# A decode kernel of four layers: the last 128 outputs of wo and w4 as one full block instead of two half blocks

## The chip, the cores and the metric

The kernel runs on one core of a Trainium2 chip. Its time is the device time of that core in microseconds (us), as the median of several runs; lower is better. A profile of one execution of the program goes with it. The engines are TensorE (PE for its matmuls, PEld for its weight loads), VectorE (DVE), ScalarE (ACT), GpSimd (POOL) and SyncE (SP), which issues the loads. Sixteen DMA engines move the data.

## The reference

Eight rows of a batch (B = 8, one token each, D = 448 features) pass through four layers: attention, mixer with MLP, attention, mixer with MLP. The attention has 16 query heads of 256 features on 8 key and value heads of 4096 positions; caches and weights are the same in both passes.

```python
def _A_ref(x, k_cache, v_cache, wq, wo):
    q = (x @ wq).reshape(B, Sq, Hq, Dh).transpose(0, 2, 1, 3)
    k = jnp.repeat(k_cache, rep, axis=1)
    v = jnp.repeat(v_cache, rep, axis=1)
    p = _softmax(jnp.einsum("bhqd,bhkd->bhqk", q, k) * (Dh ** -0.5), axis=-1)
    o = jnp.einsum("bhqk,bhkd->bhqd", p, v)
    return o.transpose(0, 2, 1, 3).reshape(B, Sq, Hq * Dh) @ wo

def _B_ref(x, w1, w2, w3, w4):
    ...
    x1 = x + hs
    return x1 + _gelu(_layernorm(x1, axis=-1) @ w3) @ w4

x = x + _A_ref(_layernorm(x), A_k_cache, A_v_cache, A_wq, A_wo)
x = x + _B_ref(_layernorm(x), B_w1, B_w2, B_w3, B_w4)
x = x + _A_ref(_layernorm(x), A_k_cache, A_v_cache, A_wq, A_wo)
x = x + _B_ref(_layernorm(x), B_w1, B_w2, B_w3, B_w4)
```

With one token the kernel treats the mixer's shifted part hs as zero, so w1 and w2 aren't read. wo has 4096 rows and 448 columns, w4 has 1792 rows and 448 columns.

## The kernel before

Keys and values don't fit the on-chip memory, so both passes of attention read them from HBM, 1 MB a tile: for each batch row and each of four pairs of key and value heads (gp) four K tiles and four V tiles. Fifteen slots of 1 MB hold them. For every row eleven tiles of the first pass stay in their slots for the second pass, and a twelfth is parked in PSUM (`away`, L614, and `back`, L621), so that they are read once.

The list `items` fixes the order of all tiles of both passes; the passes of neighbouring rows are interleaved in it. For each K tile VectorE transposes the slot in place (L584), TensorE forms the scores (L594), and ScalarE takes the exponentials (L603). The transposed probabilities (L630, L637) are the weights of the PV product of each V tile (L649). After the last use of a slot, `emit_loads` lets SyncE issue the next load into it (L576); SyncE waits for the slot's last reader. Loads are issued in the order of the items.

Between the items lie the small layers of a row, written as Python generators. `step` is called twice for an item (ahead of its scores or its PV product, and after them) and advances the generators so far that `total` of their steps are spread evenly from item `at` to item `until`; the totals are written by hand in the calls of `add_gen`. A step is what lies between two `yield`s, so its instructions stand in each engine's queue where that call puts them. The generators are:

- `first_half` and `chain`, for a row after its first pass: the softmax sums and the transposed output (`half`: L412, L438, L443, L447), the product with half of wo's rows each (`add_cols`, L339), the sums into x (L468, L469), `mlp` with w3 (L357) and w4 (L339, sum at L326), and the next query (`project_q`, wq, L285).
- `first_last` and `last`: the outputs of the second pass, collected for several rows in OT2.
- `rest`: wo, w3 and w4 of rows 0 to 3 in one go (four columns a matmul), interleaved near the end.
- For rows 4 to 7, wo's product is built up in the bank `store` while the last V tiles come in (`pv_cols`, L663, then `add_cols`). The sum at L822, `mlp_hidden`, a transposition of x (L834) and w4 (L844) end the program.

x lies as columns: feature 128 f + p on partition p of column block f of the tile xT. 448 is three and a half blocks. In the kernel before, the fourth block holds features 384 to 447 twice, on partitions 0 to 63 and on 64 to 127. `rows_to_cols` (L189, L193) brings x into this form at the start. `norm` weights the sums with wv (1/448, and 0.5/448 in the fourth block, since each feature counts twice there). It writes the normalised x into xb, whose columns 3 and 4 hold the last 64 features once on the lower and once on the upper partitions, with zeros on the others (L260 for one row, L262 for more). wq and w3 store their last 64 rows split in two halves of columns, one on the lower, one on the upper partitions, and `wblk` picks column 3 or 4 accordingly. So does `add_cols`: three blocks of 128 output columns and then two of 64, both with columns 384 to 447 of the weights. Each of its matmuls loads a block of weights and multiplies one column (or four) with it:

```python
        for fc in range(5):
            lo, hi = (128 * fc, 128 * fc + 128) if fc < 3 else (384, 448)
            r = y_ps[:, fc, :] if fc < 3 else y_ps[64 * (fc - 3) : 64 * (fc - 2), 3, :]
            for i in rows:
```

It yields after every `every` blocks and after the last.

Of the kernel before, what the change touches and what calls it, by code (L numbers as in the profile page):

```python
# [17 lines left out]
def kernel(  # L18
# [27 lines left out]
    nc = tc.nc  # L46
# [86 lines left out]

    wv = consts.tile([128, 4], FP32, name="wv")
    nc.vector.memset(wv[:, 0:3], 1.0 / D)
    nc.vector.memset(wv[:, 3:4], 0.5 / D)
    one = consts.tile([128, 1], FP32, name="one")
    nc.vector.memset(one[:], 1.0)
    ones = one[:].to_broadcast([128, 128])
# [9 lines left out]
    def xbs(nb):  # L149
        return xb[1] if nb == 1 else xb[Bn][:, :, :nb]  # L150
# [33 lines left out]
    def rows_to_cols(row, nb):  # L184

        idn = identb[:nb, :nb]
        ps = room_ps("y", nb)[:, 0 : 4 * nb].rearrange("p (f b) -> p f b", b=nb)
        for fc in range(3):
            nc.tensor.matmul(  # L189
                ps[:, fc, :], row[:nb, 128 * fc : 128 * fc + 128], idn, start=True, stop=True  # L190
            )
        for r in range(2):
            nc.tensor.matmul(  # L193
                ps[64 * r : 64 * r + 64, 3, :], row[:nb, 384:448], idn, start=True, stop=True
            )
        return ps

    def norm(x, nb, twice):

        def room(name, shape, at):
            n = shape[0] * shape[1]
            if nb < Bn:
                t = chn.tile([128, n * MID], FP32, tag=name)
                ap = t[:, 0 : n * nb]
            else:
                ap = scratch(at, n * nb)
            return ap.rearrange("p (s f b) -> p s f b", s=shape[0], f=shape[1])

        def bc(ap):
            return ap.unsqueeze(1).to_broadcast([128, 4, nb])

        xx = room("xx", (2, 4), 0)
        nc.vector.tensor_mul(xx[:, 0], x, wv[:].unsqueeze(2).to_broadcast([128, 4, nb]))
        nc.vector.tensor_mul(xx[:, 1], xx[:, 0], x)
        xs = room("xs", (1, 2), 512)[:, 0]
        nc.vector.tensor_reduce(
            xs, xx.rearrange("p s f b -> p s b f"), mybir.AxisListType.X, ALU.add
        )  # L220
        yield
        st = room_ps("st", nb).rearrange("p (s b) -> p s b", b=nb)
        nc.tensor.matmul(st, ones, xs, start=True, stop=True)  # L223
        yield
        mv = room("mv", (1, 2), 528)[:, 0]
        nc.vector.tensor_copy(mv, st)
        var = room("var", (1, 1), 608)[:, 0, 0]
        if nb == 1:
            nc.vector.scalar_tensor_tensor(
                var, mv[:, 0], mv[:, 0], mv[:, 1], ALU.mult, ALU.subtract, reverse1=True  # L230
            )
        else:
            nc.vector.tensor_mul(var, mv[:, 0], mv[:, 0])
            nc.vector.tensor_sub(var, mv[:, 1], var)


        ve = room("ve", (1, 2), 544)[:, 0]
        n = 2 if twice else 1
        nc.vector.tensor_scalar(ve[:, 0], var, 0.0, EPS, ALU.max, ALU.add)
        if twice:  # L240
            nc.vector.tensor_scalar(ve[:, 1], var, 0.0, EPS * EPS / (1 + EPS), ALU.max, ALU.add)
        rs = room("rs", (1, 2), 560)[:, 0]
        nc.gpsimd.tensor_tensor(  # L243
            rs[:, 0:n].rearrange("p n b -> p (n b)"),
            ve[:, 0:n].rearrange("p n b -> p (n b)"),
            nhalf[:].to_broadcast([128, n * nb]),
            ALU.pow,
        )
        xc = room("xc", (1, 4), 576)[:, 0]
        nc.vector.tensor_tensor(xc, x, bc(mv[:, 0]), ALU.subtract)  # L250
        yield
        if nb > 1:
            yield
        c = (1 + EPS) ** -0.5 if twice else 1.0
        rl = rs[:, n - 1]
        parts = ((slice(0, 128), 0, 3, 0), (slice(0, 64), 3, 4, 3), (slice(64, 128), 3, 4, 4))
        for pp, f0, f1, to in parts:
            dst = xbs(nb)[pp, to : to + f1 - f0, :]
            if nb == 1:
                nc.vector.tensor_scalar(dst, xc[pp, f0:f1], rl[pp], c, ALU.mult, ALU.mult)  # L260
            else:
                nc.vector.scalar_tensor_tensor(  # L262
                    dst,
                    xc[pp, f0:f1],
                    c,
                    rl[pp].unsqueeze(1).to_broadcast([pp.stop - pp.start, f1 - f0, nb]),
                    ALU.mult,
                    ALU.mult,
                )
        if twice and nb == 1:  # L270
            nc.vector.scalar_tensor_tensor(x, xc, rs[:, 0], x, ALU.mult, ALU.add)
        elif twice:
            nc.vector.tensor_tensor(xc, xc, bc(rs[:, 0]), ALU.mult)
            nc.vector.tensor_add(x, x, xc)
        yield
# [51 lines left out]

    def add_cols(y_ps, rhs, w, rows, every, open=None):

        for fc in range(5):  # L330
            lo, hi = (128 * fc, 128 * fc + 128) if fc < 3 else (384, 448)
            r = y_ps[:, fc, :] if fc < 3 else y_ps[64 * (fc - 3) : 64 * (fc - 2), 3, :]
            for i in rows:
                if open is None:
                    start, stop = i == rows[0], i == rows[-1]
                else:
                    start = open[0] and fc == 0 and i == rows[0]
                    stop = open[1] and i == rows[-1]
                nc.tensor.matmul(  # L339
                    r,  # L340
                    w[:, i, lo:hi],
                    rhs(i),
                    start=start,
                    stop=stop,
                    skip_group_check=open is not None,
                )
            if fc % every == every - 1 or fc == 4:
                yield

    def mlp_hidden(b0, nb):  # L350
# [366 lines left out]
    first_of = {}  # L717
# [4 lines left out]
    for idx, it in enumerate(items):  # L722
        n, kv, c = it
        ps, b, gp = tasks[n]
        if (ps, b, gp, kv, c) == (0, Bn - 1, REST, 0, 0):
            assert pairs_done[1, MID - 1] == 4
            add_gen("rest", 0, rest(), idx + 1, idx + 18, 25)
        p = where[(b, gp), (kv, c)] if ps == 1 and (stays(it) or inside(it)) else where[it]
        slot = slots[p]
        final = (ps, b) == (1, Bn - 1)  # L730
# [33 lines left out]
        else:  # L764
# [6 lines left out]
            if final and gp in free:  # L771
                pv_cols(oc, slot, c, gp)
                if c % 2 == 1:

                    u = c // 2
                    scale_o(oc, rz_gp, gp, u, OT2[:, :, :, b])
                    h0 = 8 * gp + 4 * u
                    run(
                        add_cols(
                            st["y"],  # L780
                            lambda i: OT2[:, i % 2, i // 2, MID:],
                            wo_sb,
                            range(h0, h0 + 4),
                            5,
                            open=(claim(st), gp == free[-1] and u == 1),
                        )
                    )
            else:
                g8 = gp // 2
                if ("o", g8) not in st:  # L790
                    while len(in_use) == 2:
                        step(10 * len(items))
                    st["o", g8] = next(t for t in o_banks if all(t is not u for u in in_use))
                    in_use.append(st["o", g8])
                pv(st["o", g8], slot, c, gp, begin=(ps, b, g8) not in begun)
                begun.add((ps, b, g8))
                if ps == 0 and inside(it):
                    away(slot)
            if c == 3:
                done = pairs_done[ps, b] = pairs_done.get((ps, b), 0) + 1  # L800
                if done == 2 and ps == 0:
                    add_gen("chain", b, first_half(b, st), idx + 1, idx + 21, 11)
                elif done == 2:
                    add_gen("chain" if final else "last", b, first_last(b, st), idx + 1, idx + 13, 9)
                elif done == 4 and ps == 0:
                    add_gen("chain", b, chain(b, st), idx + 1, first_of[(1, b), 0] - 1, 40)
                elif done == 4 and not final:
                    add_gen("last", b, last(b, st), idx + 1, idx + (7 if b == Bn - 2 else 13), 6)
        if not (ps == 0 and stays(it)):
# [18 lines left out]
    run(mlp_hidden(MID, Bn - MID))  # L828
    for q in range(4):
        for fc in range(4):  # L830
            w = 128 if fc < 3 else 64
            lo, hi = max(W * q, 128 * fc), min(W * q + W, 128 * fc + w)
            if lo < hi:
                nc.tensor.matmul(  # L834
                    o_row[32 * q : 32 * q + Bn, lo - W * q : hi - W * q],
                    xT[:w, fc, :],
                    ident2[:w, lo - 128 * fc : hi - 128 * fc],
                    start=(lo == W * q),
                    stop=False,
                    skip_group_check=True,  # L840
# [47 lines left out]
```

## Time and profile before

| what | value |
|---|---|
| median of six runs | 1119.39 us (1114.99 to 1124.4) |
| the profiled execution | 1118.35 us, of it 1116.6 us span |
| mean granted TensorE clock | 0.622 of full speed |
| read from HBM | 446.77 MB, 400 GB/s over the span |
| loads of K tiles and V tiles | 200 and 216, of 1 MB each |
| median from issue to landing | 11.1 us (K), 10.6 us (V) |
| transposes of K tiles (L584), busy | 469.3 us, 400 of 1219 ns |
| scores (L594), busy | 285.3 us |
| PV products (L649), busy | 250.1 us |
| add_cols (L339), weight loads | 2230, of them 892 of 64 columns |
| SyncE's wait for slots: on L584, L649, L594 | 217.2, 208.0, 147.0 us |

Profile lines name the line of the kernel, the engine, the operation, the tiles, a count, and times in us or, where marked, ns. A time window gives the busy time of each engine in it, the granted clock, the share of the DMA engines that was busy, and the rate. The timeline merges like instructions that follow each other; what stands in brackets is the engine's idle time before them and what ended it. Matmuls are pipelined, so that their single durations overlap: how long a run of them takes is read from the length of the run.

### The profile page before, as it was taken

The page shows a single profiled execution, that of the slowest core. Times are in us where ns is not written, and L with a number is a line of the kernel's source. Part 1 is how long each engine was busy: PE and PEld are TensorE (multiplying, and loading weights), DVE is VectorE, ACT ScalarE, POOL GpSimd, SP SyncE. Part 2 cuts the span into 40 slices and gives each one's busy share as a digit, 9 for nine tenths or more (in the row PEclk, how much of TensorE's full clock was granted, in tenths as well). Part 3 has the DMA queues.
Part 4 walks back from the last instruction along what each step waited for, and adds up shares of the span by engine and source line. Part 5 has one row for each costly group of instructions (what it writes and reads, how often), then busy time and mean ns, then how long its engine had stood idle before and what let it go on. Part 6 is the DMA issues. An engine that isn't in the chain of part 4 may idle for free. (4 is left out here: it accounts for less than half of the span.)

```text
span 1116.6 us, 36998 instructions
## 1 busy us (share of the span) xinstructions
PE 714.7 (64%) x17173; PEld 517.6 (46%) x17173; DVE 591.6 (53%) x1009; ACT 124.3 (11%) x362; POOL 15.6 (1%) x25
## 2 busy tenths in 40 slices
PE   3135567756774578636865477844777477877775
PEld 2123356534552455424553255623555355655565
DVE  5155554645375564555465464655637463485462
ACT  0001001110111011100011001101111101011010
POOL 0000000000000000000000000000000000000000
PEclk9999999655565555655566555655556555565575
DMA  9999999999999999999999999999999999999994
GB/s 359 383 420 419 412 377 401 420 411 380 395 421 420 393 406 416 418 421 395 417 419 419 421 398 417 419 420 413 409 414 418 416 408 418 418 364 410 420 419 166
DMA packets 65193, 449.15 MB, mean 402 GB/s; under 512 B 6920, under 2 KB 10896, under 8 KB 11408
## 3 DMA queue, kind: packets, MB, share of 16 engines
q1 hardware_dynamic: 65008, 446.80, 98.0%
q8 instruction: 134, 2.20, 0.8%
q14 instruction: 19, 0.16, 0.0%
q10 hardware_dynamic: 32, 0.00, 0.0%
HBM read 446.77 MB, written 0.01 MB: 400 GB/s over the span
## 5 line engine op out<-in xcount | busy, mean ns | idle before, releaser
L584 DVE STREAM_TRANSPOSE slot<-slot 128x1024 uint32<-128x1024 uint32 x400 | 469.3, 1219 | 259.8 <-DMA slot<-in_A_k_cache_dram 257.3
L594 PE MATMUL sc<-slot,qbd 128*8 128x128 bf16 x8192 | 285.3, 291 | 317.0 <-DVE slot L584 249.7
L594 PEld LDWEIGHTS <-qbd 128*8 128x8 bf16 x8192 | 191.7, 107 | 388.5 <-issue 213.7
L649 PE MATMUL o<-slot,ptw 128*8 128x256 bf16 x3968 | 250.1, 396 | 39.0 <-DMA slot<-in_A_v_cache_dram 29.7
L603 ACT ACTIVATE p_n<-sc 128x256 bf16<-128x256 f32 x128 | 95.5, 746 | 806.1 <-PE sc L594 806.1
L649 PEld LDWEIGHTS <-ptw 128*8 128x8 bf16 x3968 | 112.0, 111 | 79.5 <-issue 45.5
L339 PEld LDWEIGHTS <-wo_sb 128*128 128x128 bf16 (+1 forms) x1600 | 65.4, 123 | 25.7 <-issue 25.4
L339 PE MATMUL misc<-OT,wo_sb 128*128 128x1 bf16 (+1 forms) x1280 | 58.1, 176 | 2.1 <-issue 2.1
L285 PEld LDWEIGHTS <-wq_sb 128*128 128x128 bf16 x1152 | 34.7, 104 | 24.1 <-issue 18.5
L285 PE MATMUL misc<-xb,wq_sb 128*128 128x1 bf16 x1024 | 33.5, 166 | 3.4 <-ACT ptw L637 2.8
L637 ACT CAST ptw<-misc 128x128 bf16<-128x128 f32 x64 | 17.6, 274 | 147.8 <-PE misc L630 82.5
L603 ACT ACTIVATION_READ_ACCUMULATOR p_n<-sc 128x1 f32 x128 | 33.6, 263 | 0.0
L311 DVE TENSOR_SCALAR qbd<-misc,quad 128x64 bf16<-128x64 f32 x64 | 13.8, 278 | 34.7 <-PE misc L305 34.7
L443 PEld LDWEIGHTS misc<-R,o_sb 128*128 128x128 f32 x124 | 26.9, 300 | 9.3 <-issue 7.2
L339 PEld LDWEIGHTS <-w_sb 128*128 128x128 bf16 (+1 forms) x630 | 25.0, 125 | 11.0 <-issue 11.0
L443 PE MATMUL misc<-R,o_sb 128*128 128x8 f32 x124 | 29.8, 350 | 0.0
L243 POOL TENSOR_TENSOR t<-t,nhalf 128x2 f32<-128x2 f32 (+2 forms) x18 | 13.3, 739 | 1087.3 <-DVE t L250 1087.3
L357 PEld LDWEIGHTS <-w_sb 128*128 128x128 bf16 x560 | 18.3, 105 | 18.1 <-issue 18.1
L415 DVE RECIPROCAL rz<-misc 128x8 f32<-128x8 f32 (+1 forms) x33 | 6.3, 190 | 38.4 <-PE misc L412 36.9
L357 PE MATMUL misc<-xb,w_sb 128*128 128x1 bf16 (+1 forms) x560 | 19.2, 166 | 11.1 <-DVE xb L260 7.8
L339 PE MATMUL misc<-HT_t,w_sb 128*128 128x1 bf16 (+1 forms) x560 | 23.4, 177 | 1.7 <-DVE HT_t L380 1.7
L294 DVE CAST qT<-misc 128x32 bf16<-128x32 f32 x8 | 1.5, 192 | 41.6 <-PE misc L285 32.7
(94 smaller groups left out, 271.0 us busy)
## 6 DMA issues: line engine op xcount, KB each, us to landing
slot<-in_A_v_cache_dram SPq DMA_DIRECT2D x216, 1024.0 KB, 10.6
slot<-in_A_k_cache_dram SPq DMA_DIRECT2D x200, 1024.0 KB, 11.1
wo_sb<-in_A_wo_dram SPq DMA_DIRECT2D x1, 3584.0 KB, 25.5
wq_sb<-in_A_wq_dram SPq DMA_DIRECT2D x3, 1024.0 KB, 6.9
w_sb<-in_B_w_dram SPq DMA_DIRECT2D x1, 1568.0 KB, 15.9
w_sb<-in_B_w_dram SPq DMA_DIRECT2D x3, 448.0 KB, 25.4
wq_sb<-in_A_wq_dram SPq DMA_DIRECT2D x2, 256.0 KB, 9.9
w_sb<-in_B_w_dram SPq DMA_DIRECT2D x2, 112.0 KB
```

Source lines behind the costliest of these rows:

```text
L243: nc.gpsimd.tensor_tensor(rs[:, 0:n].rearrange("p n b -> p (n b)"), ve[:, 0:n].rearrange("p n b -> p (n b)"), nhalf[:].to_broadcast([128, ...
L285: nc.tensor.matmul(q_ps[:, j * Hq + h, :], w, xbs(nb)[:, xi, :], start=(fc == 0), stop=(fc == 3),)
L311: nc.vector.tensor_scalar_mul(qbd[:, :, :, a, :], qs.rearrange("p e (f g u h) -> p (e f) u g h", f=2, u=2, h=2)[:, :, u], quad[:, a : a + 1],)
L339: nc.tensor.matmul(r, w[:, i, lo:hi], rhs(i), start=start, stop=stop, skip_group_check=open is not None,)
L357: nc.tensor.matmul(h_ps[:, c * nb : c * nb + nb], w, xbs(nb)[:, xi, :], start=(fc == 0), stop=(fc == 3),)
L415: nc.vector.reciprocal(rz[:], z_ps)
L443: nc.tensor.matmul(ot_ps[:, j], o_sb[:].rearrange("p (i j) -> p j i", j=2)[:, j], R[:], start=True, stop=True)
L584: nc.vector.transpose(w, w)
L594: nc.tensor.matmul(sc[32 * k : 32 * k + 8, 128 * x : 128 * x + 128], qbd[:, ep, gp].rearrange("p a h -> p (a h)"), kv[:, k, 2 * half + e2, ...
L603: nc.scalar.activation(p_sb[:, :, :, 2 * u : 2 * u + 2].rearrange("p t i x -> p x t i"), sc[:, 256 * u : 256 * u + 256].rearrange("p (x t ...
L637: nc.scalar.copy(ptw[:, :, :, 6:8], pt_ps.rearrange("p t k (a h) -> p a (t k) h", a=4),)
L649: nc.tensor.matmul(o_ps[32 * q : 32 * q + 8, 0:256], ptz[:, at : at + 8], v[:, y * Dh : (y + 1) * Dh], start=(begin and y < 4), stop=(y >= ...
```

## The change

The fourth block of x becomes the features 320 to 447: its partitions 64 to 127 hold 384 to 447, and its partitions 0 to 63 hold 320 to 383, which the third block has on its upper partitions already. `rows_to_cols` needs four matmuls of 128 columns instead of three and two of 64. wv is zero on the lower partitions of the fourth block and 1/448 on the upper. In `norm` both copies of the last 64 features in xb come from partitions 64 to 127, so one operation reads the upper partitions and writes the lower ones. `add_cols` has four full blocks; the last one takes columns 320 to 447 of wo or w4. The transposition at the end reads all 128 partitions of the fourth block, against an identity that picks the upper 64. The totals of the generators are lowered by the steps that fall away. The tiles of wq and w3, all loads and the order of the items stay.

```diff
-    nc.vector.memset(wv[:, 3:4], 0.5 / D)
+    nc.vector.memset(wv[0:64, 3:4], 0.0)
+    nc.vector.memset(wv[64:128, 3:4], 1.0 / D)
...
-        for fc in range(3):
-            nc.tensor.matmul(
-                ps[:, fc, :], row[:nb, 128 * fc : 128 * fc + 128], idn, start=True, stop=True
-            )
-        for r in range(2):
-            nc.tensor.matmul(
-                ps[64 * r : 64 * r + 64, 3, :], row[:nb, 384:448], idn, start=True, stop=True
-            )
+        for fc in range(4):
+            at = min(128 * fc, D - 128)
+            nc.tensor.matmul(ps[:, fc, :], row[:nb, at : at + 128], idn, start=True, stop=True)
...
-        parts = ((slice(0, 128), 0, 3, 0), (slice(0, 64), 3, 4, 3), (slice(64, 128), 3, 4, 4))
-        for pp, f0, f1, to in parts:
-            dst = xbs(nb)[pp, to : to + f1 - f0, :]
+        parts = ((0, 128, 0, 0, 3, 0), (0, 64, 64, 3, 4, 3), (64, 128, 64, 3, 4, 4))
+        for p0, p1, x0, f0, f1, to in parts:
+            pp = slice(x0, x0 + p1 - p0)
+            dst = xbs(nb)[p0:p1, to : to + f1 - f0, :]
...
-        for fc in range(5):
-            lo, hi = (128 * fc, 128 * fc + 128) if fc < 3 else (384, 448)
-            r = y_ps[:, fc, :] if fc < 3 else y_ps[64 * (fc - 3) : 64 * (fc - 2), 3, :]
+        for fc in range(4):
+            at = min(128 * fc, D - 128)
...
-                    r,
-                    w[:, i, lo:hi],
+                    y_ps[:, fc, :],
+                    w[:, i, at : at + 128],
...
-            if fc % every == every - 1 or fc == 4:
+            if fc % every == every - 1 or fc == 3:
...
-            add_gen("rest", 0, rest(), idx + 1, idx + 18, 25)
+            add_gen("rest", 0, rest(), idx + 1, idx + 18, 23)
...
-                    add_gen("chain", b, first_half(b, st), idx + 1, idx + 21, 11)
+                    add_gen("chain", b, first_half(b, st), idx + 1, idx + 21, 10)
...
-                    add_gen("chain", b, chain(b, st), idx + 1, first_of[(1, b), 0] - 1, 40)
+                    add_gen("chain", b, chain(b, st), idx + 1, first_of[(1, b), 0] - 1, 38)
...
-                    xT[:w, fc, :],
-                    ident2[:w, lo - 128 * fc : hi - 128 * fc],
+                    xT[:, fc, :],
+                    ident2[:, lo - at : hi - at],
```

The add_cols of the last rows, whose `every` was 5, has 4 and so still yields once.

More of the change, by code (lines that the diff above doesn't have):

```diff
@@ L265, in norm @@
                     c,
-                    rl[pp].unsqueeze(1).to_broadcast([pp.stop - pp.start, f1 - f0, nb]),
+                    rl[pp].unsqueeze(1).to_broadcast([p1 - p0, f1 - f0, nb]),
                     ALU.mult,
@@ L783 @@
                             range(h0, h0 + 4),
-                            5,
+                            4,
                             open=(claim(st), gp == free[-1] and u == 1),
@@ L830 @@
         for fc in range(4):
-            w = 128 if fc < 3 else 64
-            lo, hi = max(W * q, 128 * fc), min(W * q + W, 128 * fc + w)
+            at = min(128 * fc, D - 128)
+            lo, hi = max(W * q, 128 * fc), min(W * q + W, at + 128)
             if lo < hi:
```

## The prediction

> **What bounds the kernel now.** I read the page's first parts, then the queue table, the chain of waits, the bandwidth in windows, and the timeline of the places where it falls.
>
> ```profile
> PE 714.7 (64%) x17173; PEld 517.6 (46%) x17173; DVE 591.6 (53%) x1009; ACT 124.3 (11%) x362; POOL 15.6 (1%) x25
> ...
> q1 hardware_dynamic: 65008, 446.80, 98.0%
> ...
> 1102.32 0.04 issue
> 1102.36 1.03 PE store L663 x32
> ...
> 1103.63 0.86 PE store L339 x20
> ```
>
> The first line is the busy time of the engines, the second the load queue (packets, MB, share of the sixteen DMA engines), the others pieces of the chain that ended last. No compute engine is over 64%; the load queue holds the DMA engines 98% of the span. The chain waits for V tiles until 1102.32 us, and only some 14 us of arithmetic follow. Work on TensorE is therefore worth nothing unless it lies in that tail or makes a load start late. Do loads start late? The windows (time, busy time of PE, PEld, DVE, ACT, POOL, granted TensorE clock, DMA share, GB/s):
>
> ```profile
> 380.00:390.00 10.00, 8.25 (x170) 6.19 (x168) 5.60 (x10) 1.28 (x4) 0.00 (x0) 0.50 0.92 346
> ...
> 500.00:510.00 10.00, 3.68 (x95) 2.51 (x98) 4.74 (x4) 0.38 (x1) 0.00 (x0) 0.50 1.01 419
> ...
> 980.00:990.00 10.00, 7.11 (x162) 5.17 (x165) 9.56 (x17) 0.89 (x3) 0.00 (x0) 0.50 0.95 372
> 990.00:1000.00 10.00, 8.46 (x236) 5.96 (x229) 8.83 (x10) 1.77 (x5) 0.00 (x0) 0.69 0.89 317
> ```
>
> A quiet stretch runs at 419 GB/s; while the small layers of a batch row are interleaved, it falls. Against 420 GB/s, a window loses its length times (1 - rate/420). Summed over windows of 1 us: 130 to 200 us lose 4.6, 240 to 310 lose 4.8, 380 to 430 lose 3.0, 510 to 550 lose 1.8, 640 to 690 lose 1.6, 770 to 830 lose 1.7, 890 to 940 lose 1.3, 980 to 1040 lose 4.4: **23.1 us**. This is all the change can get back from the loads; outside these stretches nothing is lost after the first 60 us. The reason: 11 of the 15 slots hold kept tiles at these times, so about four rotate, and SP may not refill a slot before its scores (L594) or PV product (L649) is done, which stand in TensorE's queue behind the small layers' matmuls.
>
> **What the change removes on TensorE.** In add_cols (L339) each row of wo or w4 has three blocks of 128 columns and the last 64 outputs twice, as two blocks of 64; now it has four blocks of 128. The page's mean durations overlap, so I take the spacing from one stretch of the timeline:
>
> ```profile
> 385.82 0.93 PEld L339 LDWEIGHTS <-wo_sb 128*128 128x128 bf16 x32 [0.21 <-issue]
> ...
> 390.76 0.93 PEld L339 LDWEIGHTS <-wo_sb 128*64 128x64 bf16 x16 [0.22 <-issue]
> ...
> 391.70 0.53 PEld L649 LDWEIGHTS <-ptw 128*8 128x8 bf16 x16
> ```
>
> 32 full blocks take 0.93 us, 29 ns each; 16 half blocks take the same, 58 ns each, and the PV product at 391.70 starts behind them. The two groups of half-block loads count 640 (wo) and 252 (w4), so 446 pairs become 446 full blocks: each saves 2 x 58 - 29 = 87 ns, **38.8 us** of TensorE in all. Sixteen rows of wo go from 3.25 to 1.86 us (-1.39), fourteen of w4 by -1.22; a batch row's chain of two wo halves and one w4 loses 4.0 us.
>
> Here a rule stands against the row. The Trainium skill ("TensorE: Matmul & The Clock Gate", LDWEIGHTS) makes the load time proportional to the columns, estimated as P/1.2 ns: two loads of 64 are then one of 128, and pairs would save nothing. The same page's section on weight-path modes says that fast weight load is on only for 128 weights not in fp32. The rows decide: by the first rule term one below is 0 and the change can't matter, by the rows it is 87 ns a pair. I take the rows, since both forms are from the same line, weights and clock (0.50).
>
> **Term 1, the tail.** The last add_cols is 20 matmuls on the chain, 0.86 us there: 12 x 29 + 8 x 58 ns = 0.81 us. Sixteen full ones make 0.46. Gain **0.35 us**, with nothing beside it: the add at L822 waits for them.
>
> **Term 2, the rest of rows 0 to 3 (930 to 1000 us).**
>
> ```profile
> 946.83 9.12 DVE L584 STREAM_TRANSPOSE slot<-slot 128x1024 uint32<-128x1024 uint32 x8
> ...
> 970.53 0.17 DVE L326 TENSOR_TENSOR xT<-xT,misc 128x16 f32<-128x16 f32 x1 [14.59 <-PE misc L339]
> ```
>
> VectorE stands for 14.59 us before the add of wo's result, and K tiles behind it can't be transposed. In that time TensorE works off 64 half blocks of this step and 32 of the batch row that runs beside it: 96 x 58 ns = 5.57 us, which become 48 x 29 = 1.39. So the add comes about 4.2 us sooner, and w4's 28 half blocks at 990.5 (1.62 us, to 0.41) give 1.2 more. The loads lose 3.6 us between 980 and 1000, when the slots that stood behind this add are late. 4.2 exceeds 3.6, but VectorE is 9.56 and 8.83 us busy of 10 there and catches up at its own pace, so I take three quarters: **2.7**, with ends 0 and 3.6.
>
> **Term 3, the eight chains.** 23.1 - 3.6 = 19.5 us are lost in them. Their inserted TensorE work per batch row: two softmax halves 2 x (0.50 + 0.93), add_cols 9.3 (2 x 3.25 and 14 x 203 ns), w3 1.6, wq 3.7, two statistics 1.0: 18.5 us, of which 4.0 go. The first wo half of each falls mostly where many loads are queued (440 to 450 us run at 424 GB/s), so 2.6 of some 15 count: 17 to 18% of 19.5 gives **3.4**. Ends: 0, if a late V tile never starves the queue, and 7.5, the loss that I find summed over the cycles from one K tile to the next in which half blocks run.
>
> **What is moved or added.** The totals of the step planner fall with the number of yields (11 to 10, 40 to 38, 25 to 23), so a chain still spreads over the same items; later steps shift by under one item: 10/38 of the way instead of 11/40 for w3's start. With each step go its VectorE operations; no DMA is in any step, but SP's refills wait for slots whose consumers are queued behind these matmuls. Every xT add is now issued one step sooner, two for rows with two adds. The start: a 64-row memset more (0.06 us, row of wv) and one matmul less; the first wq matmuls wait for their DMA until 13.68, which covers both. In the norm, the 64-row TENSOR_SCALAR of 208 ns reads partitions 64 to 127 and writes 0 to 63; no operation here moves across partitions so, and the same shape unshifted is the near row: I take 0, ends -0.05 and +0.2 us, and only the last norm is on the chain. At the end two of L834's 14 matmuls read 128 rows instead of 64; the row has 292 ns against 294 median, and the whole group (0.87 us from 1110.65) is done before HTw at 1112.00: nothing. If that cover went, at most 0.1.
>
> **Sum.** 0.35 + 2.7 + 3.4 = 6.45. The profiled execution took 1118.35 us (span 1116.6, 1.75 around it), so 1111.9; it is 1.04 below the median of 1119.39, for which I get **1112.9**.
>
> **Rivals.** (a) The loads hide all but the tail. For it: the half block at 390.76 delays a PV product by 0.93 us, yet the windows of 1 us from 391 to 395 run at 401 to 426 GB/s; and three quarters of the inserted work stays. Against it: SP's own waits name L594 and L649 for 355 us. Time: 1119.39 - 0.35 = 1119.0.
> (b) The sooner xT adds block VectorE. It works in order; L468 already waits 13.7 us in 8 cases (1.7 each) for add_cols. If an add now stands ahead of a K tile's transpose that it used to follow, and the tile has landed, the transpose waits for it, and its slot's refill with it. One such tile per chain costs 8 x 1.7 = 13.6, less the 6.45: 1126.5. It decides once tiles land before the add's matmuls are through. Against it: VectorE waits 257 us for K tiles, so at most adds the tile isn't there yet, and what is waited for has become shorter.
> (c) All ends together: 0.35 + 3.6 + 7.5 = 11.5, so 1107.9. It needs every late load to come from half blocks; the dip at 380 to 385 lies before any of them.
> (d) The change doesn't do what it says: full blocks in the fourth position keep a spacing of 58 ns. Then pairs still save 58 and most of (a) follows: 1118. Against it, the 32 in 0.93 us come from the same code.
>
> **Numbers.** About 0.5% (5.6 us) is what a measurement of this kernel tells from no change. My forecast 0.48 (its own range 1109 to 1116, of which 0.40 lies beyond 0.5%), (c) 0.10, (a) 0.24, (d) 0.03, (b) 0.15 (of which 0.13 slower by over 0.5%). Faster 0.50, same 0.37, slower 0.13. The range is 1106.5, under (c), to 1121, over (a); it leaves out (b).
>
> **What would show it.** Right: L339 without 128*64 forms and 29 ns apart; VectorE's wait before L326 near 10 us; the windows from 980 to 1000 over 390 GB/s, and that at 380 to 390 over 346; the tail 0.35 shorter. Wrong: TensorE's busy time falls but the windows keep their dips (a), new idle time before L584 put down to L468 or L326 (b), or the dips only move to the neighbouring steps.

## The result

The changed kernel takes 1114.97 us (median of 35 runs, 1107.78 to 1121.0) against 1119.36 us for the kernel before (72 runs, 1111.63 to 1128.42). The medians differ by 4.4 us. The ratio, taken over all runs, is **0.9956**, with a 95% interval of 0.9942 to 0.9969: 4.9 us less, with 3.5 to 6.5 in the interval; the text goes by this figure. That is a gain, just under the 0.5% that I had set as the limit of what can be told from no change.

The first profile of it is of an execution of 1119.91 us, well above its median. The changed kernel's lines are numbered three or four lower from the norm on (L335 was L339, L323 was L326, L645 and L659 were L649 and L663). First the engines and the load queue, from the page:

```profile
PE 677.5 (61%) x16726; PEld 483.9 (43%) x16726; DVE 593.0 (53%) x1010; ACT 124.3 (11%) x362; POOL 15.7 (1%) x25
...
q1 hardware_dynamic: 65008, 446.80, 98.0%
```

TensorE is 37.2 us less busy, and the load queue moves the same bytes for the same 98% of the span. The chain that ended last (start, us, what):

```profile
1104.02 0.04 issue
1104.06 1.03 PE store L659 x32
...
1105.34 0.62 PE store L335 x16
```

The chain still waits for the last V tile. The add_cols behind it is 16 matmuls in 0.62 us instead of 20 in 0.86. The timeline of one chain shows the blocks:

```profile
651.21 0.93 PEld L335 LDWEIGHTS <-wo_sb 128*128 128x128 bf16 x32 [0.22 <-issue]
...
652.15 0.53 PEld L645 LDWEIGHTS <-ptw 128*8 128x8 bf16 x16
...
653.11 0.93 PEld L335 LDWEIGHTS <-wo_sb 128*128 128x128 bf16 x32 [0.43 <-issue]
```

Four blocks of 16 rows in two pairs of 0.93 us: the fourth block costs 29 ns a row like the others. And the add of `rest` on VectorE, from the timeline:

```profile
950.00 6.87 DVE L580 STREAM_TRANSPOSE slot<-slot 128x1024 uint32<-128x1024 uint32 x6
...
965.72 0.17 DVE L323 TENSOR_TENSOR xT<-xT,misc 128x16 f32<-128x16 f32 x1 [8.85 <-PE misc L335]
```

VectorE stands still for 8.85 us instead of 14.59. The windows (columns as before: time, PE, PEld, DVE, ACT, POOL, granted clock, DMA share, GB/s):

```profile
380.00:390.00 10.00, 6.98 (x163) 4.75 (x163) 5.76 (x15) 0.74 (x2) 0.70 (x1) 0.50 0.98 371
...
980.00:990.00 10.00, 6.86 (x156) 4.95 (x148) 8.46 (x14) 0.99 (x3) 0.00 (x0) 0.50 1.01 418
990.00:1000.00 10.00, 6.71 (x215) 4.59 (x213) 9.54 (x11) 1.78 (x5) 0.00 (x0) 0.84 1.00 402
```

The dip at 980 to 1000 us is all but gone (372 and 317 GB/s before). Yet this execution's span is 1.5 us longer than the one of before: elsewhere it lost more. So single profiles don't decide here, and I summed each one's losses over windows of 1 us (its length times 1 - rate/420), up to 1090 us:

| profile | span | lost to 1090 us | span less loss | 130 to 980 | 980 to 1000 |
|---|---|---|---|---|---|
| before | 1116.6 | 30.3 | 1086.3 | 19.3 | 3.6 |
| before, again (e8) | 1120.2 | 34.2 | 1086.0 | 20.5 | 3.4 |
| changed | 1118.1 | 32.0 | 1086.1 | 22.0 | 0.5 |
| changed, again (e7) | 1111.7 | 25.6 | 1086.1 | 17.3 | 0.5 |

**Span less loss is the same to 0.3 us in all four.** Most of this is arithmetic: all four load the same 446.8 MB, which take 1063.8 us at 420 GB/s. What the profiles add is that the other 22 us don't move. So it is the shortfall of the loads' rate that scatters between executions, and that the change could reach. The sum doesn't say what causes the shortfall; the experiments have to. In the stretch of 130 to 980 us two profiles of the same kernel differ by up to 4.7 us, so single profiles settle only larger differences there; the dip at 980 to 1000 repeats to 0.2 us here.

### The profile page after: what moved, and what is told of

The parts are those of the page before. It is cut to its first block, busy times and chain, and to the rows that moved or that the text cites. A ratio compares the mean times of both kernels' runs of the same rounds, so it can differ in the third digit from the quotient of the medians.

```text
span 1118.1 us, 36086 instructions
## 1 busy us (share of the span) xinstructions
PE 677.5 (61%) x16726; PEld 483.9 (43%) x16726; DVE 593.0 (53%) x1010; ACT 124.3 (11%) x362; POOL 15.7 (1%) x25
## 5 line engine op out<-in xcount | busy, mean ns | idle before, releaser
L645 PE MATMUL o<-slot,ptw 128*8 128x256 bf16 x3968 | 249.1, 396 | 44.3 <-DMA slot<-in_A_v_cache_dram 38.4
L645 PEld LDWEIGHTS <-ptw 128*8 128x8 bf16 x3968 | 115.4, 113 | 89.0 <-issue 54.0
L335 PEld LDWEIGHTS <-wo_sb 128*128 128x128 bf16 x1280 | 38.8, 102 | 27.3 <-issue 26.9
L282 PEld LDWEIGHTS <-wq_sb 128*128 128x128 bf16 x1152 | 35.6, 104 | 25.8 <-issue 18.9
L335 PE MATMUL misc<-OT,wo_sb 128*128 128x1 bf16 x1024 | 35.1, 165 | 6.9 <-issue 6.9
L617 DVE STREAM_TRANSPOSE slot<-store 128x512 uint32<-128x512 uint32 x32 | 20.1, 685 | 6.4 <-PE sc L590 6.4
L353 PEld LDWEIGHTS <-w_sb 128*128 128x128 bf16 x560 | 17.2, 105 | 10.2 <-issue 9.0
L626 PE MATMUL misc<-identb,p_n 128*128 128x32 bf16 x256 | 18.2, 190 | 4.0 <-issue 2.8
L443 DVE CAST OT<-misc 128x16 bf16<-128x16 f32 x16 | 2.4, 153 | 33.9 <-PE misc L439 30.3
L610 DVE STREAM_TRANSPOSE store<-slot 128x512 uint32<-128x512 uint32 x32 | 20.0, 693 | 0.5
## 6 DMA issues: line engine op xcount, KB each, us to landing
w_sb<-in_B_w_dram SPq DMA_DIRECT2D x3, 448.0 KB, 25.6
```

The costliest lines, as they stand in the source:

```text
L282: nc.tensor.matmul(q_ps[:, j * Hq + h, :], w, xbs(nb)[:, xi, :], start=(fc == 0), stop=(fc == 3),)
L335: nc.tensor.matmul(y_ps[:, fc, :], w[:, i, at : at + 128], rhs(i), start=start, stop=stop, skip_group_check=open is not None,)
L353: nc.tensor.matmul(h_ps[:, c * nb : c * nb + nb], w, xbs(nb)[:, xi, :], start=(fc == 0), stop=(fc == 3),)
L610: nc.vector.transpose(store[n][:].bitcast(U32), slot[:].bitcast(U32)[:, 512 * n : 512 * n + 512])
L617: nc.vector.transpose(slot[:].bitcast(U32)[:, 512 * n : 512 * n + 512], store[n][:].bitcast(U32))
L626: nc.tensor.matmul(pt_ps[:, t], p_sb[:, t].rearrange("p i x -> p (i x)"), cols, start=True, stop=True,)
```

## The experiments

All but e8 are built on the changed kernel. Theory: half blocks on TensorE delay the reuse of slots, so that the load queue runs dry. Rivals: the layout or the step count carries the difference; the chains' losses have another cause than TensorE's time.

**Half blocks in the new layout (e1).** All of the change but its full block:

```diff
-            for i in rows:
+            for h in range(2 if fc == 3 else 1):
+                cols = slice(at + 64 * h, at + 64 * h + 64) if fc == 3 else slice(at, at + 128)
+                to = y_ps[64 * h : 64 * h + 64, fc, :] if fc == 3 else y_ps[:, fc, :]
+                if h == 1 and every == 1:
+                    yield
+                for i in rows:
...
-            add_gen("rest", 0, rest(), idx + 1, idx + 18, 23)
+            add_gen("rest", 0, rest(), idx + 1, idx + 18, 25)
```

> The new layout of x (features 320 to 447 in the fourth block), but the fourth block of wo and w4 again as two blocks of 64 columns, with the old number of steps (11, 40, 25). If the gain comes from TensorE's time alone, it is gone: within 2 us of the kernel before, L335's half blocks 58 ns apart, and the dip at 980 to 1000 us back at some 3.6 us lost. If the layout or the shifted norm carries the gain, it stays near -5 us.

Measured: ratio to before 1.0003 (0.9976 to 1.0031). The half blocks are 58 ns apart again (L335 has become L340 in this edit), and the dip is back; from the timeline and the windows of e1:

```profile
389.62 0.93 PEld L340 LDWEIGHTS <-wo_sb 128*64 128x64 bf16 x16 [0.21 <-issue]
```

```profile
980.00:990.00 10.00, 7.61 (x169) 5.68 (x166) 8.08 (x17) 1.43 (x5) 0.00 (x0) 0.50 0.94 374
990.00:1000.00 10.00, 8.96 (x238) 6.50 (x238) 8.83 (x12) 1.12 (x4) 0.00 (x0) 0.57 0.80 291
```

They lose 4.2 us, as in the kernel before. The gain goes with the block form; the layout of x and the shifted norm are worth nothing that shows within 3 us.

**Where it is gained (e2, e3 and e3 again, e11).** The condition `fc == 3` becomes `fc == 3 and y_ps.shape[2] > 1` in e2 (half blocks in `rest` and the last rows only), with the old total of `rest`, and `fc == 3 and y_ps.shape[2] == 1` in e3 (half blocks in the chains only), with the old totals of the chains.

> Full blocks only in the chains of single rows (32 of the 38.8 us saved on TensorE); two half blocks for rest and for the last rows. If a microsecond saved counts alike everywhere, some -4 us (4.9 x 32/38.8). If the chains' loads were hidden anyway and the gain lies in rest and the tail, within 1.5 us of the kernel before, with the dip at 980 to 1000 us as before.

> The other way about: full blocks in rest and in the last rows (6.8 of the 38.8 us), two half blocks in the chains. By the sum of the prediction -3 us (0.35 for the tail and 2.7 for rest); if the chains carry the gain, -0.5 to -1 us. The dip at 980 to 1000 us goes from 3.6 us to under 1 in either case.

> e3 once more (full blocks in rest and the last rows, half blocks in the chains), for a closer figure of the chains' own share: the changed kernel less this one. By term 3 the changed kernel is 3.4 us faster than this; if term 3 was too large, under 2 us.

Measured: e2 0.9964 (0.9938 to 0.9989), e3 0.9972 (0.9949 to 0.9994), e11 0.9990 (0.9959 to 1.0021). e2 gains some 4.0 us. The two measurements of e3 average to 0.9981, some 2.1 us, with an uncertainty of nearly the same size. The gain of e2 is clear of zero, that of e3 only just, and by their times e2 might gain it all. The dip, which scatters less, shows a part for each. From the timelines, VectorE's wait in e2 and then in e3:

```profile
963.27 0.17 DVE L323 TENSOR_TENSOR xT<-xT,misc 128x16 f32<-128x16 f32 x1 [12.18 <-PE misc L340]
```

```profile
965.58 0.17 DVE L323 TENSOR_TENSOR xT<-xT,misc 128x16 f32<-128x16 f32 x1 [12.28 <-PE misc L340]
```

Each stands between the 14.6 of before and the 8.9 of the change (14.76 and 10.44 in their second profiles), and each loses 1.9 us in the dip (e11: 1.2). TensorE's queue ahead of this add holds half blocks of `rest` and of the last row's first half, and to remove one kind shortens the wait by its part.

**More of the same (e4).** Each block as two halves, `for h in range(2)` for every fc, with the steps of the changed kernel.

> Each of the four blocks as two half blocks, the steps as in the changed kernel: 3 x 446 more pairs at 87 ns over e1's, so some 116 us more TensorE than the kernel before and 155 more than the changed one. If the loads pay for TensorE's time in proportion (4.9 us for 38.8), about +15 us against before. If slack hides most of it, under +5 us; if delays beyond the slack count in full, +30 us or more.

Measured: 1.0326 (1.0291 to 1.0360), 36.5 us slower than before. Its timeline has four half blocks of 16 rows ahead of one PV product, and its page has the busy times:

```profile
387.05 2.93 PEld L338 LDWEIGHTS <-wo_sb 128*64 128x64 bf16 x64 [0.21 <-issue]
```

```profile
PE 780.2 (67%) x18510; PEld 590.8 (51%) x18510; DVE 592.2 (51%) x1010; ACT 124.2 (11%) x362; POOL 15.6 (1%) x25
```

My count of 116 us was too high. These 64 half blocks are 46 ns apart and not 58: by the starts in the trace most come 53 ns after each other, but the first few behind each change to the other half less than 30. The page has 65.5 us more of PE and 73.2 more of PEld than before. So an added microsecond costs 0.5 us or somewhat more, where a removed one brought 4.9/38.8 = 0.13. The windows of 130 to 980 us lose 41 us instead of 19 or 20. Of the three figures it is the steepest, over 30 us, that came out, and with less added time than it was worked out for. The slack that hides most of what the change removes is used up here.

**Less of it (e9, e10).** More than half of what is left of the chains' TensorE work is taken away.

```diff
 def add_cols(y_ps, rhs, w, rows, every, open=None):
 
+        if y_ps.shape[2] == 1:
+            rows = rows[:1]
```

> The changed kernel with one row of weights instead of 14 or 16 in each block of the chains' add_cols: the sums over wo's and w4's other rows are left out, with some 4.9 us of TensorE per batch row, 39 us in all, a little more than the change itself took out of the chains (32 us). If the chains' losses follow TensorE's time as the prediction's term 3 has it, another 3 to 4 us are gained (-8 to -9 us against before); if term 3 was too large and the chains starve for another reason, at most 1 to 2 us more than the changed kernel's -4.9.

In e10 besides, in w3 and wq:

```diff
-            for fc in range(4):
+            nf = 1 if nb == 1 else 4
+            for fc in range(nf):
...
-                    stop=(fc == 3),
+                    stop=(fc == nf - 1),
```

> As e9, and of w3 and wq only the first of four blocks of features in the chains (the sums over the other features are left out): some 4 us less again per batch row, 32 us in all. What is left in a chain is the softmax sums, the transposed outputs, the statistics and VectorE's small operations. If TensorE's time is what starves the queue, the losses of the chains fall from some 18 us to under 8 and the time to some -14 us. If they stay over 13 us, the rest of the chain does it.

Measured: e9 0.9956 (0.9925 to 0.9987), the changed kernel's own ratio; e10 0.9934 (0.9903 to 0.9964), some 7.4 us under before. From e10's page:

```profile
PE 606.5 (55%) x14246; PEld 412.9 (37%) x14246; DVE 593.1 (53%) x1010; ACT 124.3 (11%) x362; POOL 15.7 (1%) x25
```

71 us less of TensorE than the changed kernel bring 2.5 us more by the ratios, uncertain by some 3.7, where 9 were expected; and the stretch of 130 to 980 us still loses 17.0 us in e10's profile. A window of it:

```profile
380.00:390.00 10.00, 5.11 (x102) 3.05 (x102) 5.90 (x16) 0.77 (x2) 0.70 (x1) 0.50 0.98 378
```

TensorE is busy half of the window, and the rate is 378 against 371 with all the matmuls. **Most of the chains' loss is not TensorE's time.**

**The order of the steps (e5, e6).** In e5 a second `yield` behind the fourth block restores the old totals. In e6 no step stands between the scores and the PV product:

```diff
-            step(idx)
             if final and gp in free:
                 pv_cols(oc, slot, c, gp)
...
         emit_loads()
+        if kv == 0 and idx + 1 < len(items) and items[idx + 1][1] == 1:
+            continue
         step(idx)
+        if kv == 1:
+            step(idx)
+            step(idx)
```

> The changed kernel with an empty step behind each fourth block, and the old totals (11, 40, 25): full blocks, the old placing of all other steps. If only TensorE's time counts, it is as fast as the changed kernel (-5 us against before). If the placing of the steps helps or harms, it differs from it by over 3 us: slower if the shorter step count was part of the gain, faster if issuing the sums into x sooner costs something (rival b).

> The changed kernel, but no step between the scores of a K tile and the PV product of the V tile that follows: these steps run behind the PV product. If what starves the load queue is that V slots are released late because matmuls of the small layers stand ahead of their PV product, the losses in the chains fall by a half or more: -8 us or more against the kernel before. If it is the K tile's path (landing, transpose, scores, release) that starves it, nothing is won, and steps that now stand ahead of the scores may cost up to 5 us.

Measured: e5 0.9954 (0.9931 to 0.9977), e6 0.9959 (0.9933 to 0.9986): both as the changed kernel. The step count does nothing that shows within some 3 us. It may have a part in the dip, though: in e5's profile the add of `rest` waits longer than in the changed kernel's two, and the dip loses 1.2 us instead of 0.5, a difference as large as that between e3 and e11.

```profile
970.51 0.17 DVE L323 TENSOR_TENSOR xT<-xT,misc 128x16 f32<-128x16 f32 x1 [11.50 <-PE misc L335]
```

The edit of e6 did what it was meant to: SyncE's wait for the PV products (L645) fell from 162.3 and 168.6 us in the changed kernel's profiles to 110.5. To release V slots sooner doesn't help, with the steps that then stand ahead of the next scores included. So the theory in its simplest form, late V slots, falls for the ordinary chains.

**Second profiles (e7, e8)** are in the table above.

> The changed kernel once more, for a second profile. The first one lay above the kernel's median. If the loads' losses scatter from run to run and the rest of the span is fixed, span less losses is again 1086 us, and the dip at 980 to 1000 us is again under 1 us.

> The kernel before once more, for a second profile. Span less losses again 1086 us; the dip at 980 to 1000 us again 3 to 4 us if it is the kernel's and not this one execution's.

Both fulfilled it.

**One slot more in rotation (e12).** If neither TensorE's time nor the order of the steps makes the rest of the loss, is it the number of slots?

```diff
-    kept = [(GP - 1, kv, n) for n in range(4) for kv in range(2)] + [(GP - 2, 0, n) for n in range(3)]
+    kept = [(GP - 1, kv, n) for n in range(4) for kv in range(2)] + [(GP - 2, 0, n) for n in range(2)]
```

> The changed kernel with ten kept tiles a row instead of eleven, so that five slots rotate instead of four, and eight tiles of 1 MB are read twice: 8.39 MB, 20.0 us at 420 GB/s. If the losses of the chains come from there being only four slots to refill, they fall from some 20 us to under 8, and the time is near 1120 us. If they have another cause, they stay and the time is near 1134 us.

Measured: 1126.35 us, ratio 1.0052 (1.0025 to 1.0079), between the two figures. By the ratios that is 10.7 us over the changed kernel, for loads that cost 20.0 at 420 GB/s: some 9 us of loss are gone. All ten runs lie between 1126.04 and 1126.65 us: the scatter shrinks to 0.6 us, where ten runs of e9 and of e10 spread over 7 and 9. The load queue on its page:

```profile
q1 hardware_dynamic: 66160, 455.19, 98.4%
```

8.4 MB more, as meant. The losses to 1090 us are 17.2 instead of 25.6 and 32.0, and from 130 us on 10.4 instead of 18.9 and 25.2. Its windows:

```profile
380.00:390.00 10.00, 7.59 (x171) 5.44 (x163) 5.74 (x13) 0.74 (x2) 0.00 (x0) 0.50 0.98 386
...
980.00:990.00 10.00, 7.63 (x164) 5.65 (x160) 7.50 (x16) 1.54 (x5) 0.00 (x0) 0.50 1.02 419
990.00:1000.00 10.00, 8.47 (x230) 6.04 (x234) 8.85 (x12) 1.05 (x3) 0.00 (x0) 0.52 1.01 418
```

With five slots in rotation the losses from 130 us on are about halved, and the time repeats; the eight tiles that are read twice cost more than that brings. No version that does the whole work is clearly faster than the changed kernel.

## Why the prediction was right, and where it was not

**The bound.** Right: the loads' bytes at 420 GB/s, some 22 us that don't move, and the shortfall of the loads' rate make up every span of the two kernels.

**TensorE's saving.** 38.8 us forecast, 37.2 less busy. The spacing held, 29 ns in the changed kernel and 58 in e1, and e1 turns the gain off with it. The rule that the prediction set against the row, from the Trainium skill ("TensorE: Matmul & The Clock Gate", LDWEIGHTS), estimates P/1.2 ns for P columns. By the starts in the trace, at a granted clock of 0.50, half blocks come 53 ns apart, as the rule has it for 64 columns, and full blocks 27, where it has 107: it is the full block that the rule misses.

**Term 1, the tail, 0.35.** Too large: the chain's piece shrank by 0.24, from 0.86 to 0.62. The mis-sized step is the 58 ns for each of the eight half blocks. Here they come in two runs of four, and by the starts in the trace the first of the 20 matmuls and the last lie 0.63 us apart before and 0.44 after, 0.19 less, in both pairs of profiles. The sums of the table can't resolve such a difference.

**Term 2, rest, 2.7.** Right. The dip lost 3.6 and 3.4 us before and 0.5 twice after, 3.0 less; VectorE's wait fell by 5.7 (by 4.3 between the second profiles), where I had put 4.2. That the neighbour row's half blocks belong to it is shown by e2 and e3. A part of it may be the step count, which I had put at nothing (1.2 us in e5's dip).

**Term 3, the chains, 3.4.** Probably too large, and the step behind it is wrong. What is left of the 4.9 us for it is 4.9 - 3.0 - 0.2 = 1.7, or 0.3 to 3.3 over the interval of the 4.9. The difference between the changed kernel and e3 gives 2.8, uncertain by some 2.6, and has the neighbour's part of the dip in it, so that it doesn't rule out 3.4. In the profiles the stretch of 130 to 980 us lost 19.3 and 20.5 us before, and 22.0 and 17.3 after, so that nothing is resolved. The step that failed is the proportion, 2.6 of 15 us of TensorE for the same share of 19.5 us: e10 takes 71 us away for 2.5, some 0.03 us for each, and even with its uncertainty that is less than the 9 us of the proportion. That the sum came near the measured gain is therefore partly luck: its term 2 holds, and term 3 has a figure of the right order from a wrong step. About half of the chains' loss goes when a fifth slot rotates (e12), and TensorE's time matters where it piles up: in `rest`, and when it is multiplied (e4). What makes the other half is not shown.

**The moved steps and the small edits** at nothing: right in the time, as far as e5 and e1 can tell (to some 3 us). The shifted 64-row operation of the norm takes 216 ns where both kinds averaged 208 before.

**The rivals.** (a), the loads hide it: true of most of the chains, not of `rest`. (b), sooner adds block VectorE: it doesn't show in the time. The waits of the adds for add_cols fell from 31.0 us (L326 and L468) to 20.7 in the first profiles. Within them the wait ahead of w4's add in the eight chains did rise, from 1.5 to 10.7; with the old steps (e5) it is gone again, and the time is the same. (c), all ends together, is excluded by the time, and (d), full blocks as slow as halves, by the spacing. The time lay in the forecast's own range of 1109 to 1116.

**Open.** What starves four slots when most of a chain's large matmuls are gone (e10) isn't found. It may be the fp32 matmuls of the softmax sums and transposed outputs, VectorE's small operations, or the loads' own latency; none of these was tried alone. SyncE's timeline points to something else that no run varied. These are issues of before and then of e10:

```profile
371.12 0.33 SPq L576 DMA_DIRECT2D slot<-in_A_k_cache_dram  x1
376.10 0.33 SPq L576 DMA_DIRECT2D slot<-in_A_v_cache_dram  x1
381.08 0.33 SPq L576 DMA_DIRECT2D slot<-in_A_k_cache_dram  x1
```

```profile
366.15 0.33 SPq L576 DMA_DIRECT2D slot<-in_A_k_cache_dram  x1
371.13 0.33 SPq L576 DMA_DIRECT2D slot<-in_A_v_cache_dram  x1
376.12 0.33 SPq L576 DMA_DIRECT2D slot<-in_A_k_cache_dram  x1
```

They are the ends of series of four such gaps, one load in 5 us instead of 2.5, while every second tile used is a V tile that is kept and gives no slot back. In before, such a series ends at 129, 245, 381, 515, 647, 779 and 891 us, and the losing stretches of the prediction begin there. e10 has them too. This would fit losses that begin where the kept tiles have used up the free slots. But the chains begin near there as well, and only a run that moves the one without the other could part them.

## What to carry to other kernels

When the transfers are the bound, write the span as a fixed part and the shortfall of the loads' rate, and read the shortfall by stage, from more than one profile: a change that a busy engine's total suggests is worth only what it returns there. TensorE's time was worth some 0.03 (e10), 0.13 (the change) or 0.5 us (e4) a microsecond here, by where it lay and how much of it there already was; look for the place where an in-order engine stands behind a pile of it. And two matmuls on half of the columns cost three to four times one on all of them here (2 x 46 to 58 ns against 29): repeat some outputs, if that fills the block.

## What the runs showed that I had not expected

With a fifth slot in rotation the scatter went as well as half of the loss; why is not shown. With four, the same program took 1111.6 to 1128.4 us (before) or 1107.8 to 1121.0 (changed); with five, and 8.4 MB more to read, 1126.04 to 1126.65 in ten runs.
